# Half-row products two banks at a time, from the third step of two pairs on

## The chip, the cores and the metric

The kernel runs on one core of one Trainium2 chip. The metric is the device time of one execution in microseconds (us); the figure shown is the median of several executions. A core has TensorE (matmuls, into the eight banks of PSUM), VectorE, ScalarE, GpSimd (POOL in the profile) and SyncE (SP, which issues most of the transfers here). All data of the matmuls are bf16, the sums in PSUM f32.

## The reference

A dense layer with a GELU in between, forward and backward. With S = 2048 rows, D = 448 and F = 1792:

```python
h = jnp.einsum("bsd,df->bsf", x, w1) + b1
h = jax.nn.gelu(h, approximate=True)
out = jnp.einsum("bsf,fd->bsd", h, w2) + b2
_out, _vjp = jax.vjp(fwd, x, w1, b1, w2, b2)
return (_out, *_vjp(grad_out))
```

So besides the output the kernel returns the gradients of x, w1, b1, w2 and b2. Per block of rows it needs u = x w1 (before the GELU), q = grad_out w2^T, h = gelu(u + b1), gh = q * gelu'(u + b1); then out = h w2 + b2 and grad x = gh w1^T, and over all rows grad w1 = x^T gh, grad w2 = h^T grad_out and the two sums over rows for b1 and b2.

## The kernel before, in words

**Tiles.** The 2048 rows are four blocks (b) of 512. F is 14 tiles of 128, taken as seven pairs (p) per block; a step number f or k counts pairs over all blocks, 0 to 27. D = 448 is three full tiles of 128 rows (KF = 3) and a left-over of 64 (DL = 64). So u of one tile is three full products of 512 columns (L212) and one over 64 rows, the tail (L227); q likewise (L258, tail L234). The 64-row operands lie in the lower or the upper half of the partitions; a tail of u and a tail of q are issued in turn, one over each half.

**Units.** The output and grad x are summed over F in units: one unit is 128 rows by 448 columns, 14 products (L328) of hT by w2 or of ghT by w1^T, one PSUM bank. `pieces(budget, ...)` issues them pair by pair as far as h and gh are there. Finished units go to SBUF in `evict` (VectorE adds b2, L341; ScalarE copies grad x, L339) and from there by GpSimd's queue to memory (L342).

**PSUM.** Four banks are single (`one0` to `one3`) and two tiles hold two banks each (`two0`, `two1`). u of a pair takes two single banks, q of a pair one of the two-bank tiles. Units are put where there is room: in a single bank by `open_one`, in a two-bank tile by `open_two`.

**Order.** The order on every engine is written out by hand (a manual schedule), in the order of the calls. After a start of single pairs (pairs 0 to 7) the main loop `for n in range(nq)` takes two pairs per step, n = 0 to 9, for k = 8 + 2n and k + 1 of q and f = k + 2 and k + 3 of u. In a step ScalarE does `act_tanh(ks)`, VectorE `dve_gate(ks)` with the evictions in it; TensorE does u of both f (`pe_u_fulls`), the tails of both, q of both (`pe_q_fulls`) and then up to 28 pieces of units; ScalarE copies u out of PSUM with the bias (`copy_u`, L267), VectorE forms gh from q (`dve_gh`, L299); then come `act_square`, `act_gelu`, one eviction and `dve_cubic` for the next step. `traffic` and `stores` issue on SP's queue what a step has to move: gh turned into rows (`turn_gh`, a transposing transfer), x and g of a later block, h to memory.

**After the loop** the remaining units run two at a time, 28 pieces for each turn of the loop. Then grad w1: `gw1_full` (L566), three tiles of D for each of four groups of F tiles (the last of two), and `gw1_tail` (L577) for the 64 left-over columns of D, two products over 64 columns of the array each at once; then grad w2 (`gw2_tile`, L598).

The steps of the loop lie in the profile at: n = 0 from 53.50 us, n = 1 from 62.40, n = 2 from 71.31, n = 3 from 82.86, n = 4 from 94.56, n = 5 from 106.26, n = 6 from 117.82, n = 7 from 129.37, n = 8 from 141.07, n = 9 from 152.78.

Of the kernel before, what the change touches and what calls it, by code (L numbers as in the profile page):

```python
# [19 lines left out]
def kernel(  # L20
# [15 lines left out]
    nc = tc.nc  # L36
    P = 128
    B, S, D = x.shape
# [3 lines left out]
    NF = F // P  # L42
    KF = D // P
    DL = D - KF * P
# [3 lines left out]
    NPAIR = NF // 2  # L48
    NSTEP = NB * NPAIR
# [6 lines left out]
    FP = [1, 2, 3, 4, 5, 6, 0]  # L56
# [23 lines left out]
    w1_f = const.tile([P, KF, F], BF16, name="w1_f")  # L80
    w2T = const.tile([P, KF + 1, F], BF16, name="w2T")
    wt1 = const.tile([P, F], BF16, name="wt1")
    w2_sb = const.tile([P, NF, D], BF16, name="w2_sb")
    w1T_sb = const.tile([P, NF, D], BF16, name="w1T_sb")
# [4 lines left out]
    def one_bank(n, name):  # L89
        return psum.tile([P, SB], F32, name=name, tag=f"one{n}")  # L90

    def two_banks(n, name):
        return psum.tile([P, 2, SB], F32, name=name, tag=f"two{n}")

    xT, gT = {}, {}
# [45 lines left out]
    halves = [slice(0, SB // 2), slice(SB // 2, SB)]  # L141
# [35 lines left out]
    hT, ghT = {}, {}  # L177
    PU, PQ = {}, {}
    order_a, order_b = [0, 1, 2, 3], [0, 1]
# [4 lines left out]
    def cols(p, a):  # L184
        return slice((2 * FP[p] + a) * P, (2 * FP[p] + a + 1) * P)

    def part(store, ks):
        return store[ks[0] // 2 % len(store)][:, 2 * (ks[0] % 2):2 * (ks[-1] % 2) + 2, :]
# [11 lines left out]
        b = ks[0] // NPAIR  # L200
        return store[b][:, 2 * (ks[0] % NPAIR):2 * (ks[-1] % NPAIR) + 2, :]

    def pe_u_fulls(f):
        b, p = divmod(f, NPAIR)
        if p == 0:
            hT[b] = blk.tile([P, NF, SB], BF16, name="hT", tag="hT")
        banks = (2, 3) if f == 1 else (0, 1) if f < NSINGLE + LEAD else order_a[2 * (f % 2):2 * (f % 2) + 2]
        PU[f] = [one_bank(n, "pu") for n in banks]
        for rs in halves if f == 0 else [slice(0, SB)]:
            for a in range(2):  # L210
                for kt in range(KF):
                    nc.tensor.matmul(PU[f][a][:, rs], lhsT=w1_f[:, kt, cols(p, a)], rhs=xT[b][:, kt, rs],  # L212
                                     start=(kt == 0 and rs.start == 0), stop=False, skip_group_check=True)

    def half(up):
        return slice(DL, P) if up else slice(0, DL)

    def open_q(k):
        b, p = divmod(k, NPAIR)
        if p == 0:  # L220
            ghT[b] = blk.tile([P, NF, SB], BF16, name="ghT", tag="ghT")
        PQ[k] = two_banks(0 if k < NSINGLE else order_b[k % 2], "pq")

    def u_tail(f, a):
        b, p = divmod(f, NPAIR)
        hf = half(b not in WIDE)
        nc.tensor.matmul(PU[f][a][:], lhsT=wt1[hf, cols(p, a)], rhs=xT[b][hf, KF, :], start=False, stop=True,  # L227
                         tile_position=(hf.start, 0), skip_group_check=True)

    def q_tail(k, a, swap=False):  # L230
        b, p = divmod(k, NPAIR)
        hf = half((b in WIDE) != swap)
        g = g_swap[b] if swap else gT[b][:, 0, :]
        nc.tensor.matmul(PQ[k][:, a, :], lhsT=w2T[hf, 0, cols(p, a)], rhs=g[hf, :], start=True, stop=False,  # L234
                         tile_position=(hf.start, 0), skip_group_check=True)

    def pe_tails(fs, ks):
        cross = bool(fs) and bool(ks) and (fs[0] // NPAIR in WIDE) != (ks[0] // NPAIR in WIDE)
        for k in ks:
            open_q(k)  # L240
        us = [(f, a) for f in fs for a in range(2)]
        qs = [(k, a) for k in ks for a in range(2)]
        if not us and len(ks) == 2:
            for a in range(2):
                q_tail(ks[0], a)
                q_tail(ks[1], a, swap=True)
            return
        for n in range(max(len(us), len(qs))):
            if n < len(us):
                u_tail(*us[n])  # L250
            if n < len(qs):
                q_tail(*qs[n], swap=cross)

    def pe_q_fulls(k):
        b, p = divmod(k, NPAIR)
        for a in range(2):
            for kt in range(1, KF + 1):
                nc.tensor.matmul(PQ[k][:, a, :], lhsT=w2T[:, kt, cols(p, a)], rhs=gT[b][:, kt, :], start=False, stop=(kt == KF),  # L258
                                 skip_group_check=True)

    def copy_u(f, engines):
        p = f % NPAIR
        for a in range(2):
            bias = b1T[:, 2 * FP[p] + a:2 * FP[p] + a + 1]
            dst = part(U4, [f])[:, a, :]
            if engines[a] == "a":
                nc.scalar.activation(out=dst, in_=PU[f][a][:], func=ACT.Identity, bias=bias)  # L267
            else:
                nc.vector.tensor_scalar(out=dst, in0=PU[f][a][:], scalar1=bias, scalar2=None, op0=ALU.add)  # L269

    def act_gelu(fs):
        for r in runs(fs):
            nc.scalar.activation(out=rows(hT, r), in_=part(U4, r), func=ACT.Gelu_apprx_tanh)  # L273

    def act_square(ks):
        nc.scalar.activation(out=part(A4, ks), in_=part(U4, ks), func=ACT.Square, scale=math.sqrt(3.0 * GELU_A * GELU_C))  # L276

    def dve_cubic(ks):
        z = part(Z4, ks)
        nc.vector.tensor_scalar(out=z, in0=part(A4, ks), scalar1=3.0 * GELU_C, scalar2=None, op0=ALU.add)  # L280
        nc.vector.tensor_tensor(out=z, in0=z, in1=part(U4, ks), op=ALU.mult)  # L281
# [16 lines left out]
    def dve_gh(k):  # L298
        nc.vector.scalar_tensor_tensor(out=rows(ghT, [k]), in0=part(Z4, [k]), scalar=1.0, in1=PQ[k][:], op0=ALU.add, op1=ALU.mult)  # L299
# [44 lines left out]
    todo = []  # L344
# [3 lines left out]
    open_units, finished = [], []  # L348

    def open_unit(ps):  # L350
        un = todo.pop(0)
        un.ps = ps
        open_units.append(un)

    def open_one():
        open_unit(one_bank(order_a[0], "ps")[:, 0:D])
        order_a.append(order_a.pop(0))

    def open_two(n, units):
        t = two_banks(n, "ps")  # L360
        for h in range(units):
            open_unit(t[:, h, 0:D])

    def pieces(budget, fmax, gmax):
        for un in list(open_units):
            while un.done < un.avail(fmax, gmax) and budget > 0:
                un.emit(un.done)
                budget -= 1
            if un.done == NPAIR:
                open_units.remove(un)  # L370
                finished.append(un)

    def evictions(most=NS):
        for un in finished[:most]:
            un.evict()
        del finished[:most]
# [48 lines left out]
    for i in range(1, NSINGLE):  # L425
        f = i + LEAD
# [24 lines left out]
    g_swap = {}  # L451
    g_low = const.tile([P, SB], BF16, name="g_low")
    nq = NSTEP // 2 - NSINGLE // 2
    for n in range(nq):
        i = NSINGLE + n
        k = NSINGLE + 2 * n
        ks = [k, k + 1]
        fs = [k + 2, k + 3] if k + 2 < NSTEP else []
        if n == 0:
            dve_cubic([k + 1])  # L460
            evictions()
        act_tanh(ks)
        dve_gate(ks, evictions)
        for f in fs:
            pe_u_fulls(f)
        pe_tails(fs, ks)
        for q in ks:
            pe_q_fulls(q)
        for f in fs:
            copy_u(f, "aa")  # L470
        for q in ks:
            dve_gh(q)
        if fs:
            open_one()
            if n == nq - 2:
                open_one()
            elif n >= 2:
                open_two(order_b[0], 1)
                order_b.reverse()
            pieces(28, k + 1, k - 1)  # L480
            act_square(fs)
            act_gelu(fs)
            evictions(1)
            dve_cubic(fs)
        if i == 8:
            nc.gpsimd.dma_start(out=g_low[0:DL, :], in_=gT[1][DL:P, 0, :])
            g_swap[1] = g_low
        if i == 15:
            nc.gpsimd.dma_start(out=g_low[DL:P, :], in_=gT[3][0:DL, 0, :])
            g_swap[3] = g_low  # L490
        traffic(i)
        stores(3, k + 1)
    stores(NSTEP, NSTEP - 1)
    while todo:
        open_one()
        open_one()
        pieces(28, NSTEP, NSTEP)
        evictions()

    x_nat = blk.tile([P, NS, D], BF16, name="x_nat", tag="hT")  # L500
    nc.sync.dma_start(out=x_nat[:], in_=x2.rearrange("(st p) d -> p st d", p=P))
# [102 lines left out]
    for ft0, n in ((0, 4), (4, 4), (8, 4), (12, 2)):  # L604
        for kt in range(KF):
            gw1_full(ft0, n, kt)
            emit_sum(3)
        if ft0 == 4:
            gw1_tail(0, 4)
        if ft0 == 12:  # L610
            gw1_tail(8, 3)
    for ft in range(NF):
        gw2_tile(ft, 2 if ft == NF - 1 else 1)
# [33 lines left out]
```

## Time and profile before

| | |
|---|---|
| median of 3 runs | 273.45 us (273.06 to 273.91) |
| the profiled execution | 272.63 us, span 270.9 us |
| granted TensorE clock | 1.00 |
| busy: PE, PEld | 266.7 us (98%) in 1444 matmuls, 130.4 us (48%) |
| busy: DVE, ACT, POOL | 175.6 us (65%), 139.4 us (51%), 38.4 us (14%) |
| steps n = 2 to 8 | 11.55 to 11.71 us each |
| the rest of the units, from n = 9 on | 152.78 to 182.5 us |
| grad w1, grad w2 | 182.5 to 225.2 us, 225.2 to 267.8 us |

How to read it: PE is TensorE's matmuls, PEld its weight loads, DVE VectorE, ACT ScalarE. A matmul's row lasts from its start to its modelled end and so overlaps the next; the pitch from start to start is what a matmul costs in a row of them. A line such as "L227 PE MATMUL pu<-xT,wt 64*128 64x512" is a matmul of source line 227 into tile pu, with weights over 64 rows and 128 columns, and 512 columns streamed. The chain of waits is listed as start, duration, engine, tile and line, "x12" for twelve in a row.

### The profile page before, as it was taken

The numbers are of one execution on the slowest core, as the hardware profiler recorded it, in microseconds if no ns is written. First come the engines' busy times: TensorE is split into PE (matmuls) and PEld (weight loads), VectorE is DVE, ScalarE is ACT, GpSimd is POOL, SyncE is SP. The second block draws the span as 40 slices with busy tenths as digits, with TensorE's granted clock in tenths as the row PEclk, the third lists the DMA queues.
The fourth block names the chain that finished last, engine by engine and source line by source line (L and its number), as shares of the span: only waits on it lengthen the run. The fifth ranks groups of instructions, "written<-read, shape, count | busy, mean of one in ns | idle before, by whom it ended". The sixth has DMA issues, their size and how long they took to land.

```text
span 270.9 us, 3726 instructions
## 1 busy us (share of the span) xinstructions
PE 266.7 (98%) x1444; PEld 130.4 (48%) x1444; DVE 175.6 (65%) x208; ACT 139.4 (51%) x163; POOL 38.4 (14%) x50
## 2 busy tenths in 40 slices
PE   8999999999999999999999999999999999999995
PEld 8344344444444545444454455554444485555554
DVE  1598999999989799676979931109999991000000
ACT  2799888799986687867768610021111121111111
POOL 1000005011001001010010111210510007900000
PEclk9999999999999999999999999999999999999999
DMA  7999899999999957075262559997111111999951
GB/s 166 215 197 259 161 209 190 289 237 176 288 221 240 237 145 180 14 186 113 77 120 81 111 120 297 376 216 193 39 40 39 41 39 34 201 216 227 203 125 34
DMA packets 112961, 44.37 MB, mean 164 GB/s; under 512 B 92032, under 2 KB 111824, under 8 KB 112944
## 3 DMA queue, kind: packets, MB, share of 16 engines
q1 hardware_dynamic: 106352, 36.43, 62.2%
q0 software_dynamic: 1824, 4.27, 5.3%
q10 hardware_dynamic: 4768, 3.44, 4.2%
q8 instruction: 11, 0.18, 0.3%
q14 instruction: 6, 0.05, 0.1%
HBM read 7.23 MB, written 14.23 MB: 79 GB/s over the span
## 4 chain that ended last, share of the span: by engine, by line
PE 88%; DVE 6%; ACT 5%; issue 0%; DVEq 0%; ACTq 0%
PE ps L328 28%; PE ps_v L598 16%; PE ps_w L566 13%; PE pq L258 12%; PE pu L212 10%; PE pu L227 4%; PE ps_w L577 2%; PE pw L172 2%; ACT A L276 1%; ACT hT L273 1%; DVE ghT L299 1%; ACT U L267 1%; PE pq L234 1%; DVE Z L296 1%; DVE A L291 1%; DVE Z L281 1%
## 5 line engine op out<-in xcount | busy, mean ns | idle before, releaser
L328 PE MATMUL ps<-w_sb,hT 128*128 128x448 bf16 x224 | 44.8, 352 | 0.0
L328 PE MATMUL ps<-w1T_sb,ghT 128*128 128x448 bf16 x224 | 43.8, 352 | 0.0
L267 ACT ACTIVATE U<-pu,b1T 128x512 bf16<-128x512 f32 x55 | 33.9, 687 | 18.2 <-PE pu L227 17.9
L598 PE MATMUL ps_v<-g_nat,h_nat 128*128 128x448 bf16 (+1 forms) x240 | 42.6, 340 | 0.0
L342 POOL DMA_DIRECT2D out_dram<-st x32 | 17.8, 558 | 162.0 <-ACT st L339 107.0
L212 PE MATMUL pu<-xT,w_f 128*128 128x512 bf16 (+1 forms) x174 | 39.9, 376 | 0.0
L258 PE MATMUL pq<-gT,w2T 128*128 128x512 bf16 x168 | 39.4, 380 | 0.0
L299 DVE SCALAR_TENSOR_TENSOR ghT<-Z,pq 128x1024 bf16<-128x1024 bf16 x28 | 33.8, 1220 | 7.2 <-PE pq L258 5.7
L566 PE MATMUL ps_w<-gh_nat,x_nat 128*128 128x512 bf16 (+1 forms) x192 | 36.7, 352 | 0.0
L285 ACT ACTIVATE Z<-Z 128x2048 bf16<-128x2048 bf16 (+1 forms) x18 | 27.5, 1528 | 10.1 <-DVE Z L281 9.9
L598 PEld LDWEIGHTS <-h_nat 128*128 128x128 bf16 x240 | 23.3, 98 | 19.3 <-issue 0.3
L328 PEld LDWEIGHTS <-hT 128*128 128x128 bf16 x224 | 21.8, 98 | 21.2 <-ACT hT L273 0.4
L328 PEld LDWEIGHTS <-ghT 128*128 128x128 bf16 x224 | 21.9, 98 | 20.9
L552 DVE TENSOR_TENSOR acc<-acc,gh_nat 128x1792 f32<-128x1792 f32 x14 | 30.0, 2142 | 0.5
L276 ACT ACTIVATE A<-U 128x1024 bf16<-128x1024 bf16 (+1 forms) x19 | 27.7, 1457 | 0.7 <-DVE U L269 0.4
L273 ACT ACTIVATE hT<-U 128x1024 bf16<-128x1024 bf16 (+1 forms) x20 | 27.7, 1390 | 0.2
L566 PEld LDWEIGHTS <-x_nat 128*128 128x128 bf16 x192 | 18.7, 98 | 17.9 <-issue 0.4
L212 PEld LDWEIGHTS <-w_f 128*128 128x128 bf16 x174 | 17.1, 100 | 19.0 <-issue 0.8
L258 PEld LDWEIGHTS <-w2T 128*128 128x128 bf16 x168 | 15.0, 98 | 23.2 <-issue 7.6
L601 ACT CAST st<-ps_v 128x448 bf16<-128x448 f32 (+1 forms) x15 | 7.6, 508 | 34.8 <-PE ps_v L598 34.8
L339 ACT CAST st<-ps 128x448 bf16<-128x448 f32 x20 | 10.3, 530 | 27.7 <-PE ps L328 27.5
L569 ACT CAST st<-ps_w 128x512 bf16<-128x512 f32 (+1 forms) x12 | 6.4, 533 | 29.9 <-PE ps_w L566 29.9
(46 smaller groups left out, 199.4 us busy)
## 6 DMA issues: line engine op xcount, KB each, us to landing
hT_dram<-hT SPq DMA_DIRECT2D x28, 256.0 KB, 3.4
out_dram<-st POOLq DMA_DIRECT2D x32, 112.0 KB, 3.2
x_nat<-in_x_dram SPq DMA_DIRECT2D x1, 1792.0 KB, 10.5
g_nat<-in_grad_out_dram SPq DMA_DIRECT2D x1, 1792.0 KB, 15.0
out_dram<-st ACTq DMA_DIRECT2D x13, 112.0 KB, 3.4
w_f<-in_w_dram SPq DMA_DIRECT2D x6, 192.0 KB, 3.9
out_dram<-st ACTq DMA_DIRECT2D x9, 128.0 KB, 1.7
w_sb<-in_w_dram SPq DMA_DIRECT2D x5, 224.0 KB, 3.8
```

The lines of the kernel that those rows point to most:

```text
L212: nc.tensor.matmul(PU[f][a][:, rs], lhsT=w1_f[:, kt, cols(p, a)], rhs=xT[b][:, kt, rs], start=(kt == 0 and rs.start == 0), stop=False, ski ...
L258: nc.tensor.matmul(PQ[k][:, a, :], lhsT=w2T[:, kt, cols(p, a)], rhs=gT[b][:, kt, :], start=False, stop=(kt == KF), skip_group_check=True)
L267: nc.scalar.activation(out=dst, in_=PU[f][a][:], func=ACT.Identity, bias=bias)
L273: nc.scalar.activation(out=rows(hT, r), in_=part(U4, r), func=ACT.Gelu_apprx_tanh)
L276: nc.scalar.activation(out=part(A4, ks), in_=part(U4, ks), func=ACT.Square, scale=math.sqrt(3.0 * GELU_A * GELU_C))
L285: nc.scalar.activation(out=z, in_=z, func=ACT.Tanh, scale=-1.0 / 3.0)
L299: nc.vector.scalar_tensor_tensor(out=rows(ghT, [k]), in0=part(Z4, [k]), scalar=1.0, in1=PQ[k][:], op0=ALU.add, op1=ALU.mult)
L328: nc.tensor.matmul(self.ps, lhsT=src[self.b][:, 2 * p + a, self.j * P:(self.j + 1) * P], rhs=w[:, 2 * FP[p] + a, :], start=(p == 0 and a = ...
L342: nc.gpsimd.dma_start(out=(out2 if self.kind == "o" else gx2)[r:r + P, :], in_=st[:, 0:D])
L552: nc.vector.tensor_tensor(out=v, in0=in0, in1=gh_nat[:, b, :, j, :], op=ALU.add)
L566: nc.tensor.matmul(ps[:, 0:n * P], lhsT=x_nat[:, st_, kt * P:(kt + 1) * P], rhs=gh_nat[:, b, ft0:ft0 + n, j, :], start=(st_ == 0), stop=(s ...
L598: nc.tensor.matmul(ps[:, 0:w], lhsT=h_nat[ft][:, st_, :], rhs=g_nat[:, st_, h * w:(h + 1) * w], start=(st_ == 0), stop=(st_ == NS - 1))
```

## The change

From the third step on (n = 2) every full product over 128 rows up to the end of the units is split into two products over 64 rows. Two banks are summed at once: `side_by_side(one, other)` issues, product by product, the lower half of one bank's sum and the upper half of another's. So each bank needs two passes, once for each half of the rows; at the second pass the two banks change halves (a turn). `half_product` records which half wrote a bank last, and where the other half follows, a no-op waits until that last product is done (in the built program the wait sits on the weight load behind it). `skip_group_check` and the start and stop flags go with the first and the last product of a bank's sum.

With it the order of a step changes, from n = 2 on: the tails come first, the later pair (f1, k1) ahead of the earlier; then q in `pe_q_rows` (first pass of k1, first pass of k0, second pass of k1, u of the *next* step's later pair, second pass of k0); `dve_gh` of k1, then of k0; then one pair of products of the next step's other u, both units in `two1` first pass, the rest of that u, the units' second pass, and the second passes of both u. `pe_u_fulls` is used up to n = 2 alone. Units are no longer fed pair by pair, but whole, two at a time. In the step n = 8 four units are opened in the single banks, two of them (`held`) with their second pass after step n = 9; the last eight run in four groups of two, the second pass of one group behind the first pass of the next. The single eviction ahead of `dve_cubic` and the early `pieces` are gone from these steps.

The left-over product of w1 for the first eight tiles, `gw1_tail(0, 4)`, moves from behind the second group to behind the last, ahead of `gw1_tail(8, 3)`.

In the built program TensorE has 1948 matmuls and as many weight loads, before 1444.

```diff
@@ -200,12 +200,16 @@
         b = ks[0] // NPAIR
         return store[b][:, 2 * (ks[0] % NPAIR):2 * (ks[-1] % NPAIR) + 2, :]
 
-    def pe_u_fulls(f):
+    def open_u(f):
         b, p = divmod(f, NPAIR)
         if p == 0:
             hT[b] = blk.tile([P, NF, SB], BF16, name="hT", tag="hT")
         banks = (2, 3) if f == 1 else (0, 1) if f < NSINGLE + LEAD else order_a[2 * (f % 2):2 * (f % 2) + 2]
         PU[f] = [one_bank(n, "pu") for n in banks]
+
+    def pe_u_fulls(f):
+        b, p = divmod(f, NPAIR)
+        open_u(f)
         for rs in halves if f == 0 else [slice(0, SB)]:
             for a in range(2):
                 for kt in range(KF):
@@ -221,18 +225,29 @@
             ghT[b] = blk.tile([P, NF, SB], BF16, name="ghT", tag="ghT")
         PQ[k] = two_banks(0 if k < NSINGLE else order_b[k % 2], "pq")
 
+    LOW, HIGH = slice(0, DL), slice(DL, P)
+    seen, count = {}, [0, 0]
+
+    def half_product(bank, ps, w, m, hf, start, stop):
+        if bank in seen and seen[bank][1] != hf.start and seen[bank][2] > count[1]:
+            turn = nc.tensor.nop()
+            tc.add_manual_dep(turn.ins, seen[bank][0], mybir.DependencyInfo(mybir.DependencyClass.Sync, mybir.DependencyReason.DATA),
+                              reason="one bank from both row halves")
+            count[1] = seen[bank][2]
+        mm = nc.tensor.matmul(ps, lhsT=w, rhs=m, start=start, stop=stop, tile_position=(hf.start, 0), skip_group_check=True)
+        count[0] += 1
+        seen[bank] = (mm.ins.name, hf.start, count[0])
+
     def u_tail(f, a):
         b, p = divmod(f, NPAIR)
         hf = half(b not in WIDE)
-        nc.tensor.matmul(PU[f][a][:], lhsT=wt1[hf, cols(p, a)], rhs=xT[b][hf, KF, :], start=False, stop=True,
-                         tile_position=(hf.start, 0), skip_group_check=True)
+        half_product(("u", f, a), PU[f][a][:], wt1[hf, cols(p, a)], xT[b][hf, KF, :], hf, False, True)
 
     def q_tail(k, a, swap=False):
         b, p = divmod(k, NPAIR)
         hf = half((b in WIDE) != swap)
         g = g_swap[b] if swap else gT[b][:, 0, :]
-        nc.tensor.matmul(PQ[k][:, a, :], lhsT=w2T[hf, 0, cols(p, a)], rhs=g[hf, :], start=True, stop=False,
-                         tile_position=(hf.start, 0), skip_group_check=True)
+        half_product(("q", k, a), PQ[k][:, a, :], w2T[hf, 0, cols(p, a)], g[hf, :], hf, True, False)
 
     def pe_tails(fs, ks):
         cross = bool(fs) and bool(ks) and (fs[0] // NPAIR in WIDE) != (ks[0] // NPAIR in WIDE)
@@ -257,6 +272,35 @@
             for kt in range(1, KF + 1):
                 nc.tensor.matmul(PQ[k][:, a, :], lhsT=w2T[:, kt, cols(p, a)], rhs=gT[b][:, kt, :], start=False, stop=(kt == KF),
                                  skip_group_check=True)
+
+    def side_by_side(one, other, part=slice(0, None)):
+        for lo, hi in zip(one(LOW)[part], other(HIGH)[part]):
+            half_product(*lo)
+            half_product(*hi)
+
+    def u_of(f, a, first=False):
+        b, p = divmod(f, NPAIR)
+        return lambda hf: [(("u", f, a), PU[f][a][:], w1_f[hf, kt, cols(p, a)], xT[b][hf, kt, :], hf, first and kt == 0, False)
+                           for kt in range(KF)]
+
+    def q_of(k, a, last=False):
+        b, p = divmod(k, NPAIR)
+        return lambda hf: [(("q", k, a), PQ[k][:, a, :], w2T[hf, kt, cols(p, a)], gT[b][hf, kt, :], hf, False, last and kt == KF)
+                           for kt in range(1, KF + 1)]
+
+    def unit_of(un, first):
+        src, w = (hT, w2_sb) if un.kind == "o" else (ghT, w1T_sb)
+        return lambda hf: [(un, un.ps, src[un.b][hf, t, un.j * P:(un.j + 1) * P], w[hf, 2 * FP[t // 2] + t % 2, :], hf,
+                            first and t == 0, not first and t == NF - 1) for t in range(NF)]
+
+    def units_side(uns, second):
+        one, other = uns[::-1] if second else uns
+        side_by_side(unit_of(one, not second), unit_of(other, not second))
+        if second:
+            for un in uns:
+                un.done = NPAIR
+                open_units.remove(un)
+                finished.append(un)
 
     def copy_u(f, engines):
         p = f % NPAIR
@@ -451,37 +495,78 @@
     g_swap = {}
     g_low = const.tile([P, SB], BF16, name="g_low")
     nq = NSTEP // 2 - NSINGLE // 2
+
+    def two_units(banks):
+        for n in banks:
+            open_unit(one_bank(n, "ps")[:, 0:D])
+        return open_units[-2:]
+
+    def pe_q_rows(ks, nxt):
+        k0, k1 = ks
+        side_by_side(q_of(k1, 0), q_of(k1, 1))
+        side_by_side(q_of(k0, 0), q_of(k0, 1))
+        side_by_side(q_of(k1, 1, True), q_of(k1, 0, True))
+        if nxt:
+            open_u(nxt[1])
+            side_by_side(u_of(nxt[1], 0, True), u_of(nxt[1], 1, True))
+        side_by_side(q_of(k0, 1, True), q_of(k0, 0, True))
+
     for n in range(nq):
         i = NSINGLE + n
         k = NSINGLE + 2 * n
         ks = [k, k + 1]
         fs = [k + 2, k + 3] if k + 2 < NSTEP else []
+        nxt = [k + 4, k + 5] if n >= 2 and k + 4 < NSTEP else []
         if n == 0:
             dve_cubic([k + 1])
             evictions()
         act_tanh(ks)
         dve_gate(ks, evictions)
-        for f in fs:
-            pe_u_fulls(f)
-        pe_tails(fs, ks)
-        for q in ks:
-            pe_q_fulls(q)
-        for f in fs:
-            copy_u(f, "aa")
-        for q in ks:
-            dve_gh(q)
-        if fs:
+        if n <= 2:
+            for f in fs:
+                pe_u_fulls(f)
+        if n < 2:
+            pe_tails(fs, ks)
+            for q in ks:
+                pe_q_fulls(q)
+            for f in fs:
+                copy_u(f, "aa")
+            for q in ks:
+                dve_gh(q)
             open_one()
-            if n == nq - 2:
-                open_one()
-            elif n >= 2:
-                open_two(order_b[0], 1)
-                order_b.reverse()
             pieces(28, k + 1, k - 1)
             act_square(fs)
             act_gelu(fs)
             evictions(1)
             dve_cubic(fs)
+        else:
+            if fs:
+                pe_tails(fs[::-1], ks[::-1])
+            for f in fs[::-1]:
+                copy_u(f, "aa")
+            pe_q_rows(ks, nxt)
+            for q in ks[::-1]:
+                dve_gh(q)
+            if nxt:
+                open_u(nxt[0])
+                side_by_side(u_of(nxt[0], 0, True), u_of(nxt[0], 1, True), slice(0, 1))
+                open_two(1, 2)
+                uns = open_units[-2:]
+                units_side(uns, False)
+                side_by_side(u_of(nxt[0], 0, True), u_of(nxt[0], 1, True), slice(1, None))
+                units_side(uns, True)
+                side_by_side(u_of(nxt[1], 1), u_of(nxt[1], 0))
+                side_by_side(u_of(nxt[0], 1), u_of(nxt[0], 0))
+            elif fs:
+                uns, held = two_units(order_a[2:4]), two_units(order_a[0:2])
+                units_side(uns, False)
+                units_side(held, False)
+                pe_tails([], [k + 2, k + 3])
+                units_side(uns, True)
+            if fs:
+                act_square(fs)
+                act_gelu(fs)
+                dve_cubic(fs)
         if i == 8:
             nc.gpsimd.dma_start(out=g_low[0:DL, :], in_=gT[1][DL:P, 0, :])
             g_swap[1] = g_low
@@ -491,11 +576,22 @@
         traffic(i)
         stores(3, k + 1)
     stores(NSTEP, NSTEP - 1)
-    while todo:
-        open_one()
-        open_one()
-        pieces(28, NSTEP, NSTEP)
-        evictions()
+    units_side(held, True)
+    evictions()
+    prev = None
+    for banks in (order_a[2:4], None, order_a[0:2], order_a[2:4]):
+        if banks is None:
+            open_two(0, 2)
+            uns = open_units[-2:]
+        else:
+            uns = two_units(banks)
+        units_side(uns, False)
+        if prev is not None:
+            units_side(prev, True)
+            evictions()
+        prev = uns
+    units_side(prev, True)
+    evictions()
 
     x_nat = blk.tile([P, NS, D], BF16, name="x_nat", tag="hT")
     nc.sync.dma_start(out=x_nat[:], in_=x2.rearrange("(st p) d -> p st d", p=P))
@@ -605,9 +701,8 @@
         for kt in range(KF):
             gw1_full(ft0, n, kt)
             emit_sum(3)
-        if ft0 == 4:
+        if ft0 == 12:
             gw1_tail(0, 4)
-        if ft0 == 12:
             gw1_tail(8, 3)
     for ft in range(NF):
         gw2_tile(ft, 2 if ft == NF - 1 else 1)
```

## The prediction

> **What bounds the kernel now.** I read the page's busy shares first, then the chain that ended last, then that chain in order of time through single steps.
>
> ```profile
> span 270.9 us, 3726 instructions
> PE 266.7 (98%) x1444; PEld 130.4 (48%) x1444; DVE 175.6 (65%) x208; ACT 139.4 (51%) x163; POOL 38.4 (14%) x50
> PE 88%; DVE 6%; ACT 5%; issue 0%; DVEq 0%; ACTq 0%
> ```
>
> The chain in order of time (start, duration, what):
>
> ```profile
> 36.20 1.23 DVE ghT L299
> ...
> 37.48 0.37 PE pq L234
> ...
> 117.82 2.59 PE pu L212 x12
> 120.41 0.32 PE pu L227
> 120.73 0.00 PE pq L234
> 120.73 0.21 PE pu L227
> 120.94 0.00 PE pq L234
> 120.94 0.21 PE pu L227
> 121.16 0.00 PE pq L234
> 121.16 0.21 PE pu L227
> 121.37 0.00 PE pq L234
> 121.38 2.70 PE pq L258 x12
> 124.07 5.30 PE ps L328 x28
> 129.37 2.59 PE pu L212 x12
> ...
> ```
>
> TensorE is the bound and, from 37.48 us on, the whole chain: a matmul follows a matmul. So only TensorE's own time counts, and any wait that reaches it. The step from 117.82 to 129.37 lasts 11.55 us. Its products have two pitches: 2.59 / 12 = 0.216 us over 512 columns, 5.30 / 28 = 0.189 us over 448. The four pairs of 64-row products (tails) go at 0.21 a pair: two products over different row halves cost one product's time. At that pitch the step is 12 x 0.216 + 4 x 0.216 + 12 x 0.216 + 28 x 0.189 = 11.34. The other 0.21 is visible twice: the first pair takes 0.32 instead of 0.21, and the twelve q products after the tails take 2.70 instead of 2.59. A change between 128-row and 64-row products costs 0.11 us each way.
>
> Some steps last longer. The busy table by step (the first and the last of the four long ones, and one of the others):
>
> ```profile
> 82.86:94.56 11.70, 11.70 (x61) 1.00 1.11 229
> 117.82:129.37 11.55, 11.55 (x61) 1.00 0.53 142
> 141.07:152.78 11.71, 11.71 (x63) 1.00 0.50 122
> ```
>
> and the timeline in the first long one (start, duration, engine, line, operation):
>
> ```profile
> 85.31 0.62 DVE L341 TENSOR_TENSOR st<-ps,b_bc 128x448 bf16<-128x448 f32 x1
> 85.38 0.39 PE L227 MATMUL pu<-xT,wt 64*128 64x512 bf16 x1
> 85.39 0.39 PE L234 MATMUL pq<-gT,w2T 64*128 64x512 bf16 x1
> ...
> 85.61 0.09 PEld L227 LDWEIGHTS <-wt 64*128 64x128 bf16 x1
> 85.61 0.38 PE L234 MATMUL pq<-gT,w2T 64*128 64x512 bf16 x1
> 85.61 0.09 PEld L234 LDWEIGHTS <-w2T 64*128 64x128 bf16 x1
> 85.83 0.38 PE L227 MATMUL pu<-xT,wt 64*128 64x512 bf16 x1
> 85.84 0.68 DVE L295 TENSOR_SCALAR Z<-Z 128x2048 bf16<-128x2048 bf16 x1
> 85.87 2.42 ACT L267 ACTIVATE U<-pu,b1T 128x512 bf16<-128x512 f32 x4 [1.19 <-PE pu L227]
> 85.98 0.37 PE L234 MATMUL pq<-gT,w2T 64*128 64x512 bf16 x1
> 86.50 1.90 PE L258 MATMUL pq<-gT,w2T 128*128 128x512 bf16 x8
> 88.01 1.22 DVE L299 SCALAR_TENSOR_TENSOR ghT<-Z,pq 128x1024 bf16<-128x1024 bf16 x1 [0.22 <-PE pq L258]
> ```
>
> The q product at 85.98 should have started beside the u product at 85.83: its bank was an output unit's and VectorE's eviction ended at 85.31 + 0.62 = 85.93. That is 0.15 us in each of the four steps of 11.70 (n = 3, 4, 7, 8). The same rows give the handovers: eviction to matmul 0.05; a product's start to VectorE's use of it: the sixth q product starts at 86.50 + 5 x 0.216 = 87.58, VectorE at 88.01, so 0.43; to ScalarE's 85.87 - 85.38 = 0.49.
>
> **The change, part by part.**
>
> Size changes. In the built program the products from the third step's tails to the last unit are one run of 1068 over 64 rows. Before, the steps n = 2 to 9 change size 16 times; now twice. The left-over products of w1 (L577) form one run instead of two, which takes 4 changes to 2. That is 16 changes fewer; at 0.107 (half of the step's 0.21, in the middle of its two visible places) 1.71 us. The left-overs agree on the size:
>
> ```profile
> 203.21 3.57 PE ps_w L577 x32
> 222.49 2.72 PE ps_w L577 x32
> L577 PE MATMUL ps_w<-gh_nat,x_nat 128*64 128x384 bf16 x32 | 2.8, 328 | 0.0
> ```
>
> 3.57 is 16 x 0.216 + 0.11; 2.72 is 16 x 0.162 + 0.13.
>
> Pairs instead of products. 504 full products (96 of q, 72 of u, 336 of units) become 504 pairs. Streamed columns are the same. A pair has two weight loads and two matmuls, four instructions in 0.216 or 0.189 us. The tails show it at 0.216 with both loads under way at 85.61, beside the products; the run of 2.72 us shows four in 0.162 us, sixteen times over, with halves of columns instead of rows. No row has 64-row pairs of 448 columns or a run of more than four, so the price is bounded: not below 0 (the columns set it), and above by the resolution of 0.01 us over three tail pitches (120.73 to 121.37 is 0.64, 0.213 each), which is 0.003 a pair or 1.5 us in all. I take 0, which the rows of sixteen bear out.
> The Trainium skill, "TensorE: Matmul & The Clock Gate", section "Measured speedup vs the span model", has a packed group last one matmul plus about 4 ns for each further tile. By that the 504 pairs would cost 2.0 us more and the sum would be +0.3; the tails' pitch of 0.21 against 0.216 does not show it as lost time, since the next pair starts a full product's pitch after the last.
>
> Turns. Each bank is now summed from both halves, and where it changes half TensorE waits for its own earlier product: 61 weight loads wait so, and everything behind them on TensorE with them. The nearest distance is two pairs (the second units' turn behind the two pairs of u; f0's tails behind f1's). The product waited for starts at 0, is seen elsewhere at 0.43, and the natural start of the waiting one is 3 x 0.216 = 0.65, or 0.62 where the first is a unit; its weights take 0.09. So 0.1 us of cover at the nearest, 0.3 at three pairs. Taken as 0 and bounded above by one size change, 0.107, for each: 6.5 us in all. It is nearest to the tails' waits, which cost nothing until the thing itself is late.
>
> Units behind dve_gh. In the steps n = 2 to 7 two units open in the second pair of banks, which held q of k+1. VectorE has to finish dve_gh(k+1) (1.22) first. From the start of q's last product: 0.43 + 1.22 + 0.05 = 1.70; TensorE has three pairs of u, three of q and one of u to do, so it arrives at 8 x 0.216 = 1.73. Cover 0.03 us: price 0, but whatever delays VectorE there is paid in full, six times. VectorE has slack before it: q's last product of k+1 starts 12 pairs (2.59) after the tails begin, where before it was 4 x 0.216 + 0.11 + 5 x 0.216 = 2.05, so 0.54 later; against that it now evicts two units in a row (0.62 more) in the four steps with output units. Even.
>
> Evictions before q's tails. Both units end together 6 pairs before the tails: the next q tail of k+1 wants the banks 0.189 + 6 x 0.216 = 1.49 after the units' last start; two evictions on VectorE end at 0.43 + 2 x 0.62 - 0.08 (rows of VectorE that don't depend on each other overlap by that: the eviction's row ends at 85.93, the next starts at 85.84) + 0.05 = 1.64. A wait of 0.15 in four steps, as now. In the two steps with units of grad x ScalarE copies them:
>
> ```profile
> L339 ACT CAST st<-ps 128x448 bf16<-128x448 f32 x20 | 10.3, 530 | 27.7 <-PE ps L328 27.5
> ```
>
> 0.49 + 2 x 0.53 = 1.55 less the like overlap, so 0 to 0.05 each. Taken as 0 for all of this.
>
> Next u between the turns. u of the next step writes banks that ScalarE still has to copy: f1's two copies end at 0.22 + 0.49 + 1.21 (half of 2.42) = 1.9 after the tails begin, wanted at 13 pairs, 2.8; f0's end about 3.1, wanted at 4.1. Hidden, with 0.9 us. Beyond that step:
>
> ```profile
> L285 ACT ACTIVATE Z<-Z 128x2048 bf16<-128x2048 bf16 x10 | 19.1, 1912 | 10.1 <-DVE Z L281 9.9
> x_nat<-in_x_dram SPq DMA_DIRECT2D x1, 1792.0 KB, 10.5
> g_nat<-in_grad_out_dram SPq DMA_DIRECT2D x1, 1792.0 KB, 15.0
> 182.49:225.21 42.72, 42.72 (x258) 22.01 (x256) 41.30 (x30) 7.51 (x14) 5.88 (x4) 1.00 0.23 64
> ```
>
> ScalarE's share of a step is 2.42 and three passes of 2048 columns near 1.91, 8.2 of 11.3 us, so the loop from copy to tanh closes. Stores, turns and loads keep their places in SP's queue, with the steps they stand in; x's and g's rows, wanted by the stretches that began at 182.49 and 225.21, are asked for when the last units that read the old hT and ghT are done, some 20 us ahead by the built order, and take 10.5 and 15.0 us to land. VectorE's sums in that stretch (41.30 busy) feed GpSimd's reductions alone, far from the end. Granted clock 1.00 throughout.
>
> Sum: -1.71 + 0 + 0 + 0 + 0 = -1.7 us. The profiled execution took 272.63 (270.9 of it the span), so 270.9; the median of the runs, 273.45, lies 0.8 above it, so 271.7.
>
> **The rivals.**
> A. Slower: a turn drains. If TensorE cannot fill the array until the product waited for has landed and the weights behind it are in, each turn costs up to a size change: 61 x 0.107 - 1.71 = +4.8, 278.2; at half of that +1.6, 275.0. It decides from 1.71 / 61 = 0.028 us a turn. For it: no row before has a wait of TensorE on itself at this distance, and the row at 85.98 shows that a waiting matmul holds back all loads behind it. Against: two to three pairs in hand.
> B. The pairs are a little longer, by 3 to 4 ns: 504 x 0.0034 = 1.7 takes all of it back, 273.4, no change. For it: the second of a pair starts up to 0.01 later (85.38 and 85.39). Against: the pitch of the tails. The page of the Trainium skill named above puts it at 4 ns.
> C. The cover of 0.03 us behind dve_gh breaks: VectorE late by one eviction (0.62) in six steps is 3.7, so 275.4. Against: 0.22 us of idle time before that row at 88.01, and 0.54 more now.
> D. The change does not take the size changes away: excluded by the built order, up to a full product that I overlooked; under 2 in 100.
>
> **How the numbers follow.** Forecast 0.62; A 0.13; B 0.13; C 0.07; the rest (several small waits that add to 1 us or more) 0.05. A measurement here tells about 0.3%, 0.82 us, from no change. The forecast's own range is 271.1 to 272.6, from the two waits at 0 instead of 0.15 x 4 to 0.8 us of small waits. Faster 0.62, same 0.19 (B, and half of the rest and of C's mild forms), slower 0.19. The range to be held 8 times in 10 takes in B and the half forms of A and C: 271.0 to 274.9.
>
> **What would show it.** In the chain, steps of 11.3 to 11.5 us instead of 11.55 to 11.70, without the 0.32 and 2.70; one 0.11 at the third step's tails and one at the first product of grad w1; the L577 groups as one run of about 6.2 us. Right for turns: the idle time of PEld at the waiting loads leaves pitches at 0.216 and 0.189. Wrong: matmul starts 0.05 or more late right behind each turn (A), pitches of 0.219 and 0.192 all along (B), the first unit product waiting for L299's row of k+1 (C).

## The result

The changed kernel takes 272.31 us (median of 9, 271.83 to 272.71) beside 273.64 us for the kernel before on the same chips: a ratio of 0.9956, 95% interval 0.9943 to 0.9970, so 1.2 us less (0.8 to 1.6). It is faster, and by less than the 1.7 us forecast. A second comparison, the run after_again, gives 272.03 us beside 273.23 and a ratio of 0.9953 (0.9933 to 0.9974).

The busy lines of the page for the changed kernel, then its chain through a step (start, duration, what). Line 237 is the matmul inside `half_product`, so the tiles tell u, q and units apart, and "x28" of ps are fourteen pairs.

```profile
span 270.5 us, 4721 instructions
PE 263.7 (97%) x1941; PEld 148.0 (55%) x1948; DVE 176.1 (65%) x208; ACT 139.3 (51%) x163; POOL 39.7 (15%) x50
```

```profile
113.83 2.65 PE ps L237 x28
116.48 0.43 PE pu L237 x4
116.91 2.65 PE ps L237 x28
119.56 1.50 PE pu L237 x13
121.06 0.01 PE pq L237
121.07 0.20 PE pu L237
...
121.70 1.96 PE pq L237 x19
123.66 0.65 PE pu L237 x6
124.31 0.65 PE pq L237 x6
124.95 0.22 PE pu L237 x2
125.17 2.65 PE ps L237 x28
```

From units to units this step takes 125.17 - 113.83 = 11.34 us, which is the bare sum of its products that the prediction gave. Fourteen pairs over 448 columns take 2.65, 0.189 each, and three pairs over 512 take 0.65, 0.216 each: a pair costs what one full product cost. The 0.32 of the first tails and the 2.70 of the q products behind them are gone, and the eight turns of the step show no time at all.

Other steps are longer. Step n = 7 in the chain, and VectorE's timeline there:

```profile
130.90 1.50 PE pu L237 x13
132.40 0.03 issue
132.43 0.37 PE pq L237
...
136.90 2.65 PE ps L237 x28
```

```profile
128.20 0.69 DVE L333 TENSOR_SCALAR A<-A 128x2048 bf16<-128x2048 bf16 x1
...
129.35 1.23 DVE L335 TENSOR_TENSOR A<-A,hT 128x2048 bf16<-128x2048 bf16 x1 [0.47 <-DVE A L333]
130.61 0.69 DVE L336 TENSOR_SCALAR A<-A 128x2048 bf16<-128x2048 bf16 x1
131.22 1.15 DVE L385 TENSOR_TENSOR st<-ps,b_bc 128x448 bf16<-128x448 f32 x2
```

136.90 - 125.17 is 11.73, 0.39 over the sum. The two evictions end at 131.22 + 1.15 = 132.37 and q's tail starts at 132.43: it is the wait of the kernel before, longer. The steps n = 3, 4 and 8 have it with 0.11, 0.12 and 0.12. Their rows of q's first tail follow; 0.01 of each stands in a step without a wait too (121.06 above):

```profile
86.81 0.12 PE pq L237
...
98.26 0.13 PE pq L237
...
144.12 0.13 PE pq L237
```

Grad w1, in the chain:

```profile
182.29 36.42 PE ps_w L662 x192
218.72 6.17 PE ps_w L673 x64
224.89 42.53 PE ps_v L694 x240
```

The left-over products take 6.17 in one run, 0.12 less than 3.57 + 2.72. The stage as a whole, from the start of its first product to the start of grad w2's first, takes 42.60 us against 42.82 (182.33 to 225.15). The 42.72 in the prediction begins later, where the chain passes from the last unit to grad w1, at 182.49.

**Where the rest went.** Spans of single executions can't be set side by side, because their start differs. The table gives, for each profiled execution but `tails_apart` (which comes last), the start of u in step n = 2 in the chain (up to there the two programs do the same), what follows from it to the first product of grad w2, where the chain shows hundredths, and what follows to the end of the span, which is known to 0.1 us:

| kernel | n = 2 at, us | from there to grad w2, us | to the end, us |
|---|---|---|---|
| before; again; a third time | 71.31; 73.36; 72.52 | 153.90; 153.90; 153.91 | 199.6; 199.5; 199.6 |
| changed; again | 72.56; 71.92 | 152.33; 152.33 | 197.9; 198.0 |
| `full_rows` | 71.69 | 153.36 | 199.0 |
| `bare_turn` | 71.34 | 153.17 | 198.9 |
| `no_cover` | 71.09 | 153.30 | 198.9 |
| `shifted` | 71.54 | 152.06 | 197.7 |
| `alternate`; again | 71.85; 72.05 | 151.59; 151.59 | 197.2; 197.2 |

The stretch to grad w2 repeats within 0.01 us for one program, while the start spreads over 2.3. So this stretch carries the attributions: the change is worth 153.90 - 152.33 = 1.57 us, of 1.71 predicted.

### The profile page after: what moved, and what is told of

It reads as the page before. It is cut to its first block, busy times and chain, and to the rows that moved or that the text cites. A ratio compares the mean times of both kernels' runs of the same rounds, so it can differ in the third digit from the quotient of the medians.

```text
span 270.5 us, 4721 instructions
## 1 busy us (share of the span) xinstructions
PE 263.7 (97%) x1941; PEld 148.0 (55%) x1948; DVE 176.1 (65%) x208; ACT 139.3 (51%) x163; POOL 39.7 (15%) x50
## 4 chain that ended last, share of the span: by engine, by line
PE 82%; SPq 12%; DMA 4%; issue 1%; ACT 0%
PE ps L237 23%; PE ps_v L694 16%; PE ps_w L662 13%; PE pq L237 9%; PE pu L237 8%; DMA w1T_sb<-in_w_dram 4%; PE ps L372 4%; SPq L129 4%; PE pu L216 3%; PE pq L273 2%; PE ps_w L673 2%; SPq L125 1%; SPq L104 1%; SPq L121 1%; SPq L122 1%; SPq L114 1%
## 5 line engine op out<-in xcount | busy, mean ns | idle before, releaser
L386 POOL DMA_DIRECT2D out_dram<-st x32 | 19.1, 602 | 161.4 <-ACT st L383 107.6
L237 PE MATMUL pq<-gT,w2T 64*128 64x512 bf16 x242 | 36.2, 376 | 0.6 <-DMA w2T<-in_w_dram 0.5
L237 PE MATMUL ps<-w1T_sb,ghT 64*128 64x448 bf16 x336 | 33.9, 349 | 0.0
L237 PE MATMUL ps<-w_sb,hT 64*128 64x448 bf16 x336 | 33.7, 349 | 0.0
L237 PEld LDWEIGHTS <-ghT 64*128 64x128 bf16 x336 | 23.5, 94 | 8.7
L237 PEld LDWEIGHTS <-hT 64*128 64x128 bf16 x336 | 20.4, 94 | 11.9
L216 PE MATMUL pu<-xT,w_f 128*128 128x512 bf16 (+1 forms) x100 | 22.6, 366 | 0.6 <-DMA xT<-in_x_dram 0.4
L237 PEld LDWEIGHTS <-w2T 64*128 64x128 bf16 x248 | 18.0, 94 | 8.7 <-DMA w2T<-in_w_dram 1.1
L237 PE MATMUL pu<-xT,w_f 64*128 64x512 bf16 x144 | 20.5, 376 | 0.0
```

The source lines that it names most:

```text
L237: mm = nc.tensor.matmul(ps, lhsT=w, rhs=m, start=start, stop=stop, tile_position=(hf.start, 0), skip_group_check=True)
L386: nc.gpsimd.dma_start(out=(out2 if self.kind == "o" else gx2)[r:r + P, :], in_=st[:, 0:D])
```

## The experiments

**The start: both kernels again.** The edit is none.

> The changed kernel as it is, for a second profile of it. In its first profile the stretch from the first u product of step n = 2 to the end is 197.9 us against 199.6 before (1.65 less, 1.71 predicted), but that product started at 72.56 instead of 71.31 us, behind a wait of 1.1 us for w1T_sb. Theory 1, the start varies from one execution to the next: this profile has its n = 2 start somewhere between 70.5 and 73, and the stretch from there again 197.7 to 198.2. Theory 2, the changed program starts later by itself: n = 2 starts at 72.3 to 72.8 again.

> The kernel before as it is, for the place of n = 2 in it. The changed kernel and its three variants so far have the first u product of step n = 2 at 72.56, 71.92, 71.85, 71.69 and 71.34 us, on code that is the same up to there; the kernel before had it at 71.31. If the start only varies, this profile has it anywhere from 71 to 72.6; if the changed program starts later by itself, at 71.3 again.

> As before_again, a third profile of the kernel before: the first u product of step n = 2 between 71 and 72.6 if the start only varies, at 71.3 if it is the program's own.

The first u products of n = 2 in the chain: the kernel before again (span 272.9 us) and a third time (272.1), then the changed one again (269.9).

```profile
73.36 2.59 PE pu L212 x12
```

```profile
72.52 2.59 PE pu L212 x12
```

```profile
71.92 0.21 PE pu L216
```

The start varies, and not by program: 71.3 to 73.4 before, 71.1 to 72.6 in the changed kernel and its variants. Theory 1 holds; the kernel before, at 73.36, was even later than the 71 to 72.6 that was named for a start that only varies. In the changed kernel's first profile the units waited 1.1 us for the transposed w1 ("PE ps L372 <- DMA w1T_sb<-in_w_dram: 1.1, 1, 1.1" among its waits), which alone hid most of the gain in that profile. The chain shows the transfer and the first products behind it:

```profile
34.54 11.47 DMA w1T_sb<-in_w_dram
...
46.05 2.82 PE ps L372 x14
```

From 46.05 to the start of n = 2 at 72.56 are 26.51 us. The chain passes through this transfer in eight of the eleven profiles of the table, and in all eight n = 2 starts 26.51 or 26.52 us behind those products, before and after the change alike. In the other three it doesn't, and n = 2 starts at 71.09 to 71.34. So the start follows the landing of this transfer; why that varies, the runs do not tell.

**Order alone: `full_rows`.** The changed kernel's order with products over 128 rows (the edit is shortened; the stop flag of a unit moves to its last product too).

```diff
 def side_by_side(one, other, part=slice(0, None)):
-    for lo, hi in zip(one(LOW)[part], other(HIGH)[part]):
-        half_product(*lo)
-        half_product(*hi)
+    for bank, ps, w, m, hf, start, stop in one(slice(0, P))[part]:
+        new = ...          # first product of this bank
+        nc.tensor.matmul(ps, lhsT=w, rhs=m, start=new, stop=stop, skip_group_check=True)
```

> The order of the changed kernel with full products over 128 rows: where two banks were summed side by side, the first pass sums one bank whole and the second the other. The tails stay over 64 rows, so 14 changes of size come back and all turns go. If the gain is the size changes: 14 x 0.107 = 1.5 us more, less up to 0.7 for the waits before q's tails, which the slower tails hide: 273.1 to 273.8, with 0.32 for the first tails' pair and 2.70 for twelve q products back in the chain. If the new order made the gain: 272.3, as the changed kernel.

Measured: 272.52 us, ratio 0.9977 (0.9958 to 0.9996), where the changed kernel has 0.9953 in the same comparison. That is 0.5 us more in the medians, below the 0.8 to 1.5 expected; in the stretch from n = 2 to grad w2 it is 153.36 - 152.33 = 1.03, inside. The chain of `full_rows` through one step:

```profile
101.92 2.65 PE ps L282 x14
...
108.94 0.32 PE pu L237
...
109.26 0.21 PE pu L237
...
113.47 2.65 PE ps L282 x14
...
132.37 0.28 PE pq L237
```

The 0.32 is back and the step takes 113.47 - 101.92 = 11.55. So half rows are worth about 1.03 and the order (with w1's left-overs) 0.54 of the 1.57. The waits before q's tails close the account. In `full_rows` only n = 7 has one, of 0.28 (the last row above); before there were four of 0.15, 0.62 in all; in the changed kernel there are 0.74. Half rows: 14 x 0.107 = 1.50 saved, less 0.74 - 0.28 = 0.46, makes 1.04. Order: 0.22 in grad w1 and 0.62 - 0.28 = 0.34, makes 0.56. Both agree with the stretches to 0.02.

**The turn without cover: `bare_turn`.**

```diff
 units_side(uns, False)
-side_by_side(u_of(nxt[0], 0, True), u_of(nxt[0], 1, True), slice(1, None))
 units_side(uns, True)
+side_by_side(u_of(nxt[0], 0, True), u_of(nxt[0], 1, True), slice(1, None))
```

> In steps n = 2 to 7 the units' second pass follows the first at once, the two pairs of u come behind it. Nothing covers the turn. If a turn waits for the product to land (seen 0.43 us after its start) and costs nothing where two pairs stand between: 0.43 + 0.05 to 0.1 - 0.19 = 0.3 us in each of six steps, 1.8 in all, 274.1, less what it gives the evictions. If a turn costs a drain wherever it stands, or nothing at all: 272.3, the same as the changed kernel.

Measured: 272.83 us, ratio 0.9967 (0.9945 to 0.9989), so 0.8 us more than the changed kernel in the medians. The chain at a turn of the units:

```profile
101.51 2.67 PE ps L237 x28
104.18 0.05 issue
104.23 2.82 PE ps L237 x28
107.05 1.73 PE pu L237 x16
```

The two passes take 107.05 - 101.51 = 5.54 instead of 5.30: a turn with nothing between costs 0.24, not quite the 0.3 expected. Six of them are 1.45; the stretch grew by 0.84, since the later tails no longer wait (of the 0.74 only 0.15 is left, in n = 7). The two pairs of u do what the prediction said: they take a cost of 0.24 to nothing. That a turn costs the same wherever it stands has fallen, by this run and by the step of 11.34 with eight turns in it.

**The cover behind dve_gh: `no_cover`.**

```diff
-side_by_side(u_of(nxt[0], 0, True), u_of(nxt[0], 1, True), slice(0, 1))
 open_two(1, 2)
 uns = open_units[-2:]
 units_side(uns, False)
-side_by_side(u_of(nxt[0], 0, True), u_of(nxt[0], 1, True), slice(1, None))
+side_by_side(u_of(nxt[0], 0, True), u_of(nxt[0], 1, True))
```

> In steps n = 2 to 7 the changed kernel without the one pair of u ahead of the units: it follows the units' first pass with the other two. dve_gh of k + 1 then has 6 pairs to run behind instead of 7. The prediction's sum: needed 1.70 us, had 1.73, now 1.51: 0.19 us in each of six steps, 1.1 in all, 273.1 beside a changed kernel of 272.0, with the first unit product behind L343 in each step. If VectorE's row was not what the units waited for, or has more slack than 0.03: up to 0.2 less per step, down to 272.0.

Measured: 272.80 us beside 273.70, ratio 0.9969 (0.9945 to 0.9992).

```profile
101.19 0.03 issue
101.21 2.83 PE ps L237 x28
104.04 0.65 PE pu L237 x6
```

With 6 pairs instead of 7 behind k + 1's last q product, the units' first pass takes 104.04 - 101.19 = 2.85 with the gap ahead of it instead of 2.65: 0.20 a step, where 0.19 was expected. So the cover is there and is thin: one pair, 0.216, hides the 0.20 with 0.02 over. In the stretch it cost 0.97, not 1.1, because in n = 7 part of it falls into the wait that is there anyway.

**The waits before q's tails: `alternate`.** In odd steps k goes ahead of k + 1, and the units take k's banks.

```diff
+turn_order = ks[::-1] if n % 2 == 0 else ks
-pe_tails(fs[::-1], ks[::-1])
+pe_tails(fs[::-1], turn_order)
 ...
-pe_q_rows(ks, nxt)
-for q in ks[::-1]:
+pe_q_rows(turn_order, nxt)      # in it: k1, k0 = ks
+for q in turn_order:
     dve_gh(q)
 ...
-open_two(1, 2)
+open_two(turn_order[0] % 2, 2)
```

> The two pairs of a step change places in every other step: odd n takes k ahead of k + 1 in tails, q and dve_gh, and its units go to the two-bank tile of k. So q's tails of the bank that held units come two pairs later in the next step. If the waits of 0.11, 0.12, 0.39 and 0.12 us in steps n = 3, 4, 7 and 8 of the changed kernel are the evictions on VectorE, they go (two pairs are 0.43): 0.7 us less than the changed kernel, 271.6. If it is something else that holds the tails (the turn of the u tails, the copies), they stay and the time is 272.3.

> The alternating order once more, beside the kernel before on the same chip. Its trace has all six steps n = 2 to 7 at 11.34 us, the bare sum of their products, 0.7 us under the changed kernel from n = 2 to the end. So 2.3 us under the kernel before if both start alike: 271.0 beside 273.3; the first measurement, a ratio of 0.9919, is 2.2.

Measured: 270.86 us, where 271.6 was expected, ratio 0.9919 (0.9889 to 0.9949), and again 271.01 beside 273.70, 0.9894 (0.9880 to 0.9909). The chain through n = 7:

```profile
124.23 2.65 PE ps L237 x28
...
131.46 0.00 PE pq L237
...
135.57 2.65 PE ps L237 x28
```

11.34 in this step too, where the changed kernel had 11.73. The waits were the evictions: two pairs more before the tail that needs the bank, and all of them go, 152.33 - 151.59 = 0.74 in the stretch, as much as the four waits together. This version is faster than both kernels: by 2.2 and 2.9 us against the one before in the two comparisons, 2.31 in the stretches. What the second comparison shows beyond that lies outside the stretch.

**The stop on VectorE: `shifted`.**

```diff
-nc.vector.memset(row0[0:1, :], 1.0)
+for _ in range(11):
+    nc.vector.memset(row0[0:1, :], 1.0)
```

> The changed kernel with ten more small writes of row0 on VectorE at the start, where it waits for b1 anyway (L174 waits until 5.3 us): every later VectorE instruction stands ten places further on in its stream. In all traces of the changed order VectorE stops for 0.4 us ahead of one and the same instruction, L335 of step n = 7, with nothing late that it waits for; in that step q's tails wait 0.39 us instead of 0.12. If the stop belongs to a place in VectorE's stream, it moves ten instructions ahead, to the end of step n = 6's gate, where VectorE has 2.2 us to spare: L335 of n = 7 follows L333 within 0.1, the tails of n = 7 wait 0.12, and the stretch from n = 2 to the end is 197.7 instead of 197.95. If the stop belongs to that instruction or its data, L335 keeps its 0.47 and the tails their 0.39.

One execution was looked at. VectorE in step n = 7 (line numbers are one higher here):

```profile
127.18 0.69 DVE L334 TENSOR_SCALAR A<-A 128x2048 bf16<-128x2048 bf16 x1
127.97 1.23 DVE L336 TENSOR_TENSOR A<-A,hT 128x2048 bf16<-128x2048 bf16 x1
129.23 0.69 DVE L337 TENSOR_SCALAR A<-A 128x2048 bf16<-128x2048 bf16 x1
129.92 1.16 DVE L386 TENSOR_TENSOR st<-ps,b_bc 128x448 bf16<-128x448 f32 x2
```

The stop is gone from that instruction, the row of q's first tail in n = 7 is down to 0.13 ("131.38 0.13 PE pq L238"), a wait of 0.12, and the stretch is 0.27 shorter, where 0.25 was expected. So the stop of 0.4 us does not belong to that instruction or its data. That it belongs to a place in VectorE's stream fits, but its new place isn't seen: no other instruction of this profile shows such a stop, and one inside the 2.17 us for which VectorE waits for q, behind the gate of n = 6, would leave no mark. Why there, the runs do not tell.

**Two runs of left-overs: `tails_apart`.**

```diff
-        if ft0 == 12:
+        if ft0 == 4:
             gw1_tail(0, 4)
+        if ft0 == 12:
             gw1_tail(8, 3)
```

> The changed kernel with w1's left-over products in two runs again, as before. One run of them took 6.17 us and grad w1 42.60 us, two took 3.57 and 2.72, and 42.82. If two changes of size more are all: grad w1 is 42.81 again, 0.21 more, and the rest of the kernel as in the changed one. If the difference came with the kernel otherwise (loads, banks), 42.60.

One execution, whose start was some 4 us late at a lower granted clock (0.993 in the mean), so only stretches behind the start are read. The busy table from the first product of grad w1 to the first of grad w2, and the chain:

```profile
185.52:228.35 42.83, 42.83 (x258) 22.04 (x257) 41.30 (x30) 8.03 (x15) 6.45 (x5) 1.00 0.41 90
```

```profile
206.41 3.57 PE ps_w L673 x32
...
225.69 2.72 PE ps_w L673 x32
```

42.83 against 42.60: two changes of size more are 0.23, and the rest of the kernel stays as it was, for the stretch from n = 2 (at 75.86 here) to grad w2 (at 228.41) is 152.55 against 152.33.

## Why the prediction was right, and what it mis-sized

**What bounds it.** Right. TensorE's chain is the time from n = 2 on, and a step without waits is the sum of its products, 11.34, to the last digit shown.

**Size changes, 1.71.** Right in mechanism and price. `tails_apart` has 0.23 for two, and the account of `full_rows` closes to 0.01 with 0.107 each. The two changes that remain stand where they were forecast: 0.32 for the first pair of tails in n = 2, and grad w1's full products take 36.42 us in the chain where `full_rows`, which comes to them from 128 rows, has 36.32.

**Pairs, 0.** Right: 0.189 and 0.216 over runs of fourteen and three pairs. Rival B, with 0.003 more a pair, would have shown 2.69 where 2.65 stands. The page of the Trainium skill that the prediction weighed, "TensorE: Matmul & The Clock Gate", section "Measured speedup vs the span model", adds about 4 ns to a group's span for each further tile. In a stream of pairs the trace shows no such loss: the next pair starts as if there had been one product.

**Turns, 0.** Right, with rival A answered by `bare_turn`: 0.24 where nothing covers it, 0 behind two pairs. The prediction's cover of 0.1 at two pairs follows from it as about 0.19 (two pairs of 0.216 less 0.24).

**Units behind dve_gh, 0.** Right, and as close as was said: 0.03 forecast, 0.02 by `no_cover`. Rival C, an eviction in VectorE's way, did not come: VectorE stood idle for 0.22 us before dve_gh of k + 1 in n = 2 and for 1.20 to 2.24 in n = 3 to 7, waiting for q.

**Evictions before q's tails.** This is the term that was mis-sized. Forecast was "a wait of 0.15 in four steps, as now", net 0. Three steps have 0.11 to 0.12, which is near; n = 7 has 0.39, because VectorE had stopped for 0.4 us shortly before and the evictions stand directly behind. Together 0.74 instead of 0.62: 0.12 less gain. No profile of the kernel before shows such a stop, so the prediction had no row for it. Without it, in `shifted`, n = 7 waits 0.12 like the others, and the four waits would have been 0.47, less than forecast. The sum becomes 1.71 - 0.12 = 1.59, and the stretches show 1.57.

**The time.** 271.7 was forecast from a median of 273.45; on the chips of the comparison the kernel before had 273.64, so the like figure is 271.9, and 272.31 was measured. Of that 0.4, 0.1 is the evictions. The ratios give 1.2 and 1.3 less, the stretches 1.57; the upper ends of the intervals (1.6 and 1.8 us) reach it. The start, which the change does not touch and which varies by 2 us, is in every timed run and in no stretch; a start that is later by the program itself was looked for and not seen (means of 72.4 before in three profiles and 71.8 in eight of the changed kernel and its variants, `tails_apart` left out). An estimate from the table: every execution's time lies some 1.8 us above its span (272.33 beside 270.5), and the medians less this and less the stretch to the end leave starts of 71.9 to 72.3 before, about 72.3 and 72.5 for the changed kernel and 71.7 to 72.2 for its variants, which share its code up to n = 2. So the 0.3 us between ratios and stretches would lie in the start; why its median came out so, stays open.

## What to carry to other kernels

Where one engine is the whole chain, count its products at the pitches of the trace, and look for what a step has beyond that sum: here 0.21 for two changes between row sizes and 0.15 for a bank that was evicted late. Splitting products into row halves cost nothing here, with two banks side by side and at least two pairs of other work (0.43 us) between the two halves of a bank. When a buffer is wanted too early by one user, give that user the later place in the order before looking for a faster eviction: alternating two pairs was worth 0.7 us here and cost no instruction.

## What was not expected of the hardware

VectorE stopped for 0.4 us ahead of one instruction, the same in both profiles of the changed kernel and in those of `full_rows`, `bare_turn`, `no_cover`, `alternate` (both) and `tails_apart`; with ten instructions more ahead of it the stop was gone from there, and the three profiles of the kernel before show none of the kind. The start of the same program varies by 2 us between executions, by when the transposed w1 lands. And two 64-row products that fall out of step after a wait keep their distance. In n = 4 VectorE's evictions end at 97.97, and q's tail starts 0.14 behind u's:

```profile
97.88 0.38 PE L237 MATMUL pu<-xT,wt 64*128 64x512 bf16 x1
98.02 0.37 PE L237 MATMUL pq<-gT,w2T 64*128 64x512 bf16 x1
98.10 0.38 PE L237 MATMUL pu<-xT,wt 64*128 64x512 bf16 x1
98.23 0.37 PE L237 MATMUL pq<-gT,w2T 64*128 64x512 bf16 x1
```

At the next pair the distance is still 0.13, and the pair comes 0.21 to 0.22 us behind the first. At the tails of the next step the two start 0.01 apart again; what brought them together isn't shown.
